# The sign of float64 weight words: from VectorE's integer operations to a parametric ReLU of ScalarE

## Chip, cores and metric

One core of one Trainium2 chip runs the kernel. The metric is the device time of one execution in microseconds (us), the median of 3 runs for the kernel before. A profile of one execution shows the five engines: PE (TensorE, its matmuls), PEld (its weight loads), DVE (VectorE), ACT (ScalarE), POOL (GpSimd) and SP (SyncE, which here only issues DMAs).

## What is computed

An attention layer and two feed-forward layers, one after the other, on 2 x 576 = 1152 tokens of width 512:

```
q_pool = q.reshape(B, H, S // 2, 2, D).mean(axis=3)          # B=2, H=8, S=1152, D=64
attn = softmax(q_pool @ k.T / sqrt(D)) ; x = attn @ v        # x: 1152 x 512
xn = x / sqrt(mean(x*x) + 1e-6) * rms_g                      # first layer, d_ff = 1536
x = (silu(xn @ w_gate) * (xn @ w_val)) @ w_out
h = x @ w_in                                                 # second layer, d_ff = 2048
out = (h * tanh(softplus(h))) @ w_out2                       # h*tanh(softplus(h)) is Mish
```

The five weight matrices (`w_gate`, `w_val`, `w_out`, `w_in`, `w_out2`) arrive as float64, everything else as float32. TensorE is given float16 pairs: each operand is split into a high and a low part, and each product is three matmuls (high x high, high x low, low x high).

## The kernel before

**Weights.** A float64 is two 32-bit words. A job (there are 68) loads a tile `raw` of 128 x 512 pairs of words, 512 KB, and turns it into the float16 pair, in four steps that lie on three engines:

- `w_a` on ACT: the high word, read as a float32 with every second word of `raw` skipped, times 2^-111, into `gx`. That leaves the sign in bit 31 and brings the exponent to where a shift by 3 puts it in float32's place.
- `w_b` on DVE, three integer operations on 128 x 512 words: L408 shifts `gx` left by 3 and masks off bit 31, L411 takes the sign bit from `gx` and ors it in, L414 shifts the low word right by 29 and ors it in. The result `c` holds the bits of the float32.
- `w_c`: ACT (L421) rounds `c` to float16 (the high part), POOL (L134) subtracts it from `c` for the low part.

The tiles `raw` have 4 buffers, `gx` and `c` 2 each. An engine works through its instructions in the order of the program. `job_step` issues `w_c` of one job, `w_b` of the next and `w_a` of the one after that, so a job crosses three steps.

**Stages.** The 72 attention steps (`attn_step`) come first: scores on PE (L249), row maximum on DVE (`m`, L267), exponential on ACT (`e`, L274), high part on ACT (L287) and low part on POOL, a DMA transpose, and five steps later the product with v on PE. From step 54 on, the first four jobs are spread over the steps by `job_piece`, one piece a step, four steps a job: `w_a` (with `w_c` of the job before), L408, L411, L414.

Then come the first layer's units (`unit1`): 24 matmuls of 288 columns for one block of 128 features and 288 tokens, ACT's Silu (L572), DVE's product `fo` (L574), ACT's high part (L581) and POOL's low part `h`. After each unit stands one `job_step`; PE can be three units ahead, since the units take two of six PSUM banks each. The jobs run out before the units do. The output matmuls of the first layer (`unit1o`, 36 matmuls each, DVE's `y` at L136 frees the bank) again have one or two job steps behind each; `w_out`'s blocks (`woh`) have two buffers, so a job for a third block waits until PE is done with the first, and what stands behind it on ACT, POOL and DVE waits too.

In the second layer's loop one step is 12 matmuls into `z`, Mish on ACT (`mo`, L648), the high part of `g` on ACT, the low part on DVE (L136), one job step while there are jobs (the 16 of `w_out2`, `w2o_job`), and from the seventh step on the output matmuls `po`. `z` has five PSUM banks.

Of the kernel before, what the change touches and what calls it, by code (L numbers as in the profile page):

```python
# [9 lines left out]
F32 = mybir.dt.float32  # L10
F16 = mybir.dt.float16
I32 = mybir.dt.int32
ACTF = mybir.ActivationFunctionType
ALU = mybir.AluOpType
# [26 lines left out]
def kernel(  # L41
# [13 lines left out]
    nc = tc.nc  # L55
# [48 lines left out]
    w2o = stretch.rearrange("p (k w d) -> p k w d", k=F2, w=2)  # L104
# [280 lines left out]
    def words(w):  # L385
        return w.bitcast(I32)
# [3 lines left out]
    def w_load(src, n):  # L390
        t = raw_p.tile([128, n, 128 * KD // n, 2], I32, tag="raw", name="raw", bufs=4)
        weng[0].dma_start(out=t, in_=src)
        return t

    def w_a(job):
        t = job["raw"]
        gx = raw_p.tile([128, t.shape[1], t.shape[2]], F32, tag="gx", name="gx")
        nc.scalar.activation(out=gx, in_=t[:, :, :, 1].bitcast(F32), func=ACTF.Copy, scale=2.0 ** -111)
        job["g"] = gx

    def w_b(job, part=None):

        t, g = job["raw"], job["g"].bitcast(I32)
        if part in (None, 0):
            job["c"] = raw_p.tile([128, t.shape[1], t.shape[2]], I32, tag="c", name="c")
        c = job["c"]
        if part in (None, 0):
            nc.vector.tensor_scalar(out=c, in0=g, scalar1=3, scalar2=0x7FFFFFFF,  # L408
                                    op0=ALU.logical_shift_left, op1=ALU.bitwise_and)
        if part in (None, 1):  # L410
            nc.vector.scalar_tensor_tensor(out=c, in0=g, scalar=-0x80000000, in1=c,  # L411
                                           op0=ALU.bitwise_and, op1=ALU.bitwise_or)
        if part in (None, 2):
            nc.vector.scalar_tensor_tensor(out=c, in0=t[:, :, :, 0], scalar=29, in1=c,  # L414
                                           op0=ALU.logical_shift_right, op1=ALU.bitwise_or)
            del job["raw"], job["g"]

    def w_c(job):
        hi, lo = job["to"]()
        cf = job.pop("c").bitcast(F32)  # L420
        nc.scalar.activation(out=hi, in_=cf, func=ACTF.Copy)  # L421
        lo_op(job.get("eng", nc.gpsimd), lo, cf, 1.0, hi)

    jobs = []
    jn = [0, 0, 0, 0]

    def job_load(upto):
        while jn[0] < min(upto, len(jobs)):
            jobs[jn[0]]["raw"] = jobs[jn[0]]["load"]()
            jn[0] += 1  # L430
# [3 lines left out]
    def job_step(k=1):  # L434

        for _ in range(k):
            if jn[3] < jn[2]:
                w_c(jobs[jn[3]])
                jn[3] += 1
            if jn[2] < jn[1]:  # L440
                w_b(jobs[jn[2]])
                jn[2] += 1
            if jn[1] < len(jobs):
                job_load(jn[1] + 1)
                w_a(jobs[jn[1]])
                jn[1] += 1
            job_load(jn[1] + AHEAD)

    def job_piece(k):

        i, p = divmod(k, 4)
        if p == 0 and i:
            w_c(jobs[i - 1])
            jn[3] += 1
        if i == NE:
            return
        if p == 0:
            w_a(jobs[i])
            jn[1] += 1
            job_load(jn[1] + AHEAD)  # L460
        elif p == 1:
            w_b(jobs[i], 0)
        else:
            w_b(jobs[i], p - 1)
            jn[2] += p == 3


    ss_t, rw = {}, {}
# [158 lines left out]
    def w2o_job(z):  # L627
        return {"load": lambda: w_load(words(w_out2)[z * 128:(z + 1) * 128, :].rearrange(
            "(k p) (f t) -> p k f t", p=128, t=2), 1),
            "to": lambda: (w2o[:, z:z + 1, 0, :], w2o[:, z:z + 1, 1, :])}  # L630

    gt, zt = {}, {}

# [123 lines left out]
    with tc.manual_schedule():  # L757
# [25 lines left out]
        for n in range(NIT):  # L783
            attn_step(n)
            if rs:
                rs.pop(0)()
            if n == RMS0:
                rs = rms_steps(0, 0, NI + 1, 2)
            if n == JOBL:
                job_load(AHEAD)  # L790
            if 0 <= n - JOB0 <= 4 * NE:
                job_piece(n - JOB0)
# [84 lines left out]
        for i, (d, c) in enumerate(outs):  # L877
# [4 lines left out]
            if i:  # L882
                unit1o_end(*outs[i - 1])
        unit1o_end(*outs[-1])
        jobs += [w2o_job(z) for z in range(F2)]
        for p in (ps_f, ps_t, ps_av, wo_p, h1_p, h0_p, ftm):
            p.release()
# [60 lines left out]
```

## Time and profile before

| | |
|---|---|
| median of 3 runs | 677.12 us (676.36 to 677.2) |
| span of the profiled execution | 674.8 us |
| what lies around the span, median less span | 2.3 us |
| PE busy | 605.0 us (90%) |
| DVE busy | 449.9 us (67%) |
| ACT busy | 392.4 us (58%) |
| POOL busy | 328.3 us (49%) |

The times are those of the page of the profile. Matmuls overlap in it (their ends are modelled), so PE's share says where it works, not whether it works at its full rate; the count of matmuls in a stretch says that. The share of DVE is an average over stages: it is near full in some stretches and near nothing in others. An engine's time includes time in which an instruction has started and waits for a port.

### The profile page before, as it was taken

Reading aid. Unit: us, or ns where it says so; the run is one execution under the profiler, and the core shown is the slowest. Engines: PE = TensorE matmul, PEld = TensorE weight load, DVE = VectorE, ACT = ScalarE, POOL = GpSimd, SP = SyncE. Lnnn points to the kernel's source line nnn. Section 1 sums busy time; section 2 is a strip of 40 time slices with the busy share of each in tenths; the row PEclk is TensorE's granted clock in tenths of the full one; section 3 lists DMA queues with packets and bytes.
Section 4 is the critical chain, followed back from the end, with each engine's and each line's share of the span. In section 5 each row is a group of like instructions: output and inputs, shape, how many; then the busy total and the mean of one; then the engine's idle time right before and its main releaser. Section 6 shows DMA issues by size and latency. Waiting matters only on the chain.

```text
span 674.8 us, 14672 instructions
## 1 busy us (share of the span) xinstructions
PE 605.0 (90%) x5880; PEld 421.6 (62%) x5880; DVE 449.9 (67%) x740; ACT 392.4 (58%) x659; POOL 328.3 (49%) x260
## 2 busy tenths in 40 slices
PE   3688888888867788899999999999999999999997
PEld 2466566666645567677777677777755555555553
DVE  3889998989969996769999922488299911111110
ACT  4888898998968887655555541344356623223221
POOL 0778878688889752467878741344133300000000
PEclk9899999999988899999999999999999999999999
DMA  6799999999998997625555512156055101001001
GB/s 190 123 211 189 186 183 185 197 182 186 204 203 163 174 161 147 132 94 157 159 157 169 158 47 63 39 182 187 17 169 159 64 0 48 1 1 32 16 1 47
DMA packets 161908, 84.05 MB, mean 125 GB/s; under 512 B 124720, under 2 KB 152368, under 8 KB 161840
## 3 DMA queue, kind: packets, MB, share of 16 engines
q1 hardware_dynamic: 151184, 67.71, 47.0%
q10 hardware_dynamic: 10656, 15.40, 8.4%
q8 instruction: 46, 0.75, 0.5%
q14 instruction: 22, 0.18, 0.1%
HBM read 50.07 MB, written 2.36 MB: 78 GB/s over the span
## 4 chain that ended last, share of the span: by engine, by line
PE 49%; DVE 28%; ACT 8%; issue 8%; DMA 4%; POOL 2%; ACTq 1%; SPq 0%; DVEq 0%; POOLq 0%
DVE m L267 8%; DVE c L411 6%; PE z L544 5%; PE z L546 5%; PE z L545 5%; PE po L681 4%; PE po L680 4%; PE po L679 4%; ACT e L274 3%; PE py L544 3%; PE py L546 3%; PE py L545 3%; DVE c L408 3%; DMA et<-hl 3%; DVE et L134 2%
## 5 line engine op out<-in xcount | busy, mean ns | idle before, releaser
L134 POOL TENSOR_TENSOR hl<-e,hl 128x768 f16<-128x768 f32 x71 | 117.5, 1655 | 60.5 <-ACT hl L287 37.0
L267 DVE TENSOR_REDUCE m<-s 128x1 f32<-128x1152 f32 x72 | 97.3, 1351 | 8.9 <-PE s L249 7.6
L274 ACT ACTIVATE e<-s,m 128x1152 f32<-128x1152 f32 x72 | 87.7, 1218 | 18.8 <-DVE m L268 17.6
L249 PE MATMUL s<-kqT 128*128 128x384 f16 (+1 forms) x480 | 87.9, 336 | 9.6 <-DVE kqT L203 7.5
L136 DVE SCALAR_TENSOR_TENSOR g<-mo,g 128x384 f16<-128x384 f32 x48 | 26.9, 562 | 100.5 <-ACT g L654 100.5
L411 DVE SCALAR_TENSOR_TENSOR c<-gx,c 128x512 int32<-128x512 int32 x68 | 75.7, 1114 | 2.2
L338 PE MATMUL av<-vv,et 128*128 128x65 f16 (+1 forms) x720 | 75.4, 195 | 1.8 <-DMA et<-hl 1.0
L134 POOL TENSOR_TENSOR stretch<-c,stretch 128x512 f16<-128x512 f32 x40 | 51.3, 1283 | 52.0 <-ACT stretch L421 51.8
L414 DVE SCALAR_TENSOR_TENSOR c<-raw,c 128x512 int32<-128x512 int32 x68 | 75.0, 1103 | 2.2
L340 PE MATMUL av<-vv,et 128*128 128x64 f16 (+1 forms) x720 | 75.3, 194 | 0.0
L341 PE MATMUL av<-vv,et 128*128 128x65 f16 (+1 forms) x720 | 75.1, 196 | 0.0
L338 PEld LDWEIGHTS <-et 128*128 128x128 f16 (+1 forms) x720 | 68.0, 102 | 3.6 <-issue 2.3
L340 PEld LDWEIGHTS <-et 128*128 128x128 f16 (+1 forms) x720 | 67.8, 101 | 0.8
L341 PEld LDWEIGHTS <-et 128*128 128x128 f16 (+1 forms) x720 | 67.8, 101 | 0.0
L134 POOL TENSOR_TENSOR h<-fo,h 128x288 f16<-128x288 f32 x48 | 48.8, 1016 | 36.3 <-ACT h L581 36.3
L648 ACT ACTIVATE mo<-z 128x384 f32<-128x384 f32 x48 | 23.3, 484 | 71.3 <-PE z L546 71.3
L287 ACT ACTIVATE hl<-e 128x768 f16<-128x768 f32 x72 | 60.7, 843 | 3.5 <-DMA et<-hl 1.4
L544 PE MATMUL z<-y,w2i 128*128 128x384 f16 x192 | 62.6, 326 | 0.0
L545 PE MATMUL z<-y,w2i 128*128 128x384 f16 x192 | 62.6, 326 | 0.0
L546 PE MATMUL z<-y,w2i 128*128 128x384 f16 x192 | 62.6, 326 | 0.0
L309 PE MATMUL ep<-idf,e 128*128 128x128 f32 x216 | 39.0, 291 | 24.7 <-ACT e L274 23.5
L249 PEld LDWEIGHTS <-kqT 128*128 128x128 f16 (+1 forms) x480 | 40.2, 102 | 33.1 <-issue 15.6
(106 smaller groups left out, 1570.0 us busy)
## 6 DMA issues: line engine op xcount, KB each, us to landing
raw<-in_moe_w_out_dram SPq DMA_DIRECT2D x28, 512.0 KB, 3.4
raw<-in_moe_w_in_dram SPq DMA_DIRECT2D x16, 512.0 KB, 3.7
raw<-in_moe_w_gate_dram SPq DMA_DIRECT2D x8, 512.0 KB, 3.6
raw<-in_moe_w_val_dram SPq DMA_DIRECT2D x8, 512.0 KB, 3.5
vn<-in_v_dram ACTq DMA_DIRECT2D x14, 288.0 KB, 2.9
kn<-in_k_dram ACTq DMA_DIRECT2D x12, 288.0 KB, 4.5
qn<-in_q_dram ACTq DMA_DIRECT2D x12, 256.0 KB, 3.4
raw<-in_moe_w_gate_dram ACTq DMA_DIRECT2D x4, 512.0 KB, 5.0
```

The source lines that it names most:

```text
L134: eng.tensor_tensor(out=out_, in0=in_, in1=hi, op=ALU.subtract)
L249: mm = nc.tensor.matmul(out=ps[p0:p0 + m, c, 0:SN], lhsT=qt[:, w * NTI + slot, p0:p0 + m], rhs=kt[:, e * NJ + c * per:e * NJ + (c + 1) * p ...
L267: nc.vector.tensor_reduce(out=m[:, 0:1], in_=ps[:, :, 0:SN], op=ALU.max, axis=AXL.XY, negate=True)
L274: nc.scalar.activation(out=e.rearrange("p (c s) -> p c s", c=SC), in_=ps[:, :, 0:SN], func=ACTF.Exp, bias=m[:, 1:2], scale=s_scale)
L338: nc.tensor.matmul(out=av[0:m, o0:o0 + D + 1], lhsT=hi, rhs=vr[:, D:2 * D + 1], start=(jj == 0), stop=False)
L340: nc.tensor.matmul(out=av[0:m, o0:o0 + D], lhsT=hi, rhs=vr[:, 0:D], start=False, stop=False)
L341: nc.tensor.matmul(out=av[0:m, o0:o0 + D + 1], lhsT=et[:, z + (NB if jj < NB else PB), p0:p0 + m], rhs=vr[:, D:2 * D + 1], start=False, st ...
L411: nc.vector.scalar_tensor_tensor(out=c, in0=g, scalar=-0x80000000, in1=c, op0=ALU.bitwise_and, op1=ALU.bitwise_or)
L414: nc.vector.scalar_tensor_tensor(out=c, in0=t[:, :, :, 0], scalar=29, in1=c, op0=ALU.logical_shift_right, op1=ALU.bitwise_or)
L544: nc.tensor.matmul(out=ps, lhsT=w0, rhs=x0, start=(i == 0), stop=False)
L545: nc.tensor.matmul(out=ps, lhsT=w0, rhs=x1, start=False, stop=False)
L546: nc.tensor.matmul(out=ps, lhsT=w1, rhs=x0, start=False, stop=(i == n - 1))
```

## The change

The 52 jobs of the first four weight matrices lose one of their three DVE operations. ACT's pass over the high word becomes a parametric ReLU: positive words are multiplied by 2^-111 as before, negative ones by 2^-111 and by -2^32, so that they come out positive with 32 added to the exponent, which is bit 28. The shift by 3 puts this bit where the sign belongs, and what was masked off and ored in needs no operation of its own. DVE's first operation now reads `raw` (the low word, shifted right by 29), its second shifts `gx` left by 3 and ors `c` in. In the attention's `job_piece` the fourth step of a job has no DVE operation any more.

The 16 jobs of `w_out2`, which run beside Mish, are marked `"mish"`: they keep ACT's plain scaled copy and get four DVE operations (low word shifted; sign masked and ored in; `gx` shifted and masked in place; the two ored).

```diff
     def w_a(job):
...
-        nc.scalar.activation(out=gx, in_=t[:, :, :, 1].bitcast(F32), func=ACTF.Copy, scale=2.0 ** -111)
+        hw = t[:, :, :, 1].bitcast(F32)
+        if job.get("mish"):
+            nc.scalar.activation(out=gx, in_=hw, func=ACTF.Copy, scale=2.0 ** -111)
+        else:
+            nc.scalar.activation(out=gx, in_=hw, func=ACTF.Prelu, scale=2.0 ** -111, alpha=-(2.0 ** 32))
     def w_b(job, part=None):
...
         if part in (None, 0):
-            nc.vector.tensor_scalar(out=c, in0=g, scalar1=3, scalar2=0x7FFFFFFF,
-                                    op0=ALU.logical_shift_left, op1=ALU.bitwise_and)
+            nc.vector.tensor_scalar(out=c, in0=t[:, :, :, 0], scalar1=29, scalar2=None,
+                                    op0=ALU.logical_shift_right)
         if part in (None, 1):
-            nc.vector.scalar_tensor_tensor(out=c, in0=g, scalar=-0x80000000, in1=c,
-                                           op0=ALU.bitwise_and, op1=ALU.bitwise_or)
-        if part in (None, 2):
-            nc.vector.scalar_tensor_tensor(out=c, in0=t[:, :, :, 0], scalar=29, in1=c,
-                                           op0=ALU.logical_shift_right, op1=ALU.bitwise_or)
+            if job.get("mish"):
+                nc.vector.scalar_tensor_tensor(out=c, in0=g, scalar=-0x80000000, in1=c,
+                                               op0=ALU.bitwise_and, op1=ALU.bitwise_or)
+                nc.vector.tensor_scalar(out=g, in0=g, scalar1=3, scalar2=0x7FFFFFFF,
+                                        op0=ALU.logical_shift_left, op1=ALU.bitwise_and)
+                nc.vector.tensor_tensor(out=c, in0=g, in1=c, op=ALU.bitwise_or)
+            else:
+                nc.vector.scalar_tensor_tensor(out=c, in0=g, scalar=3, in1=c,
+                                               op0=ALU.logical_shift_left, op1=ALU.bitwise_or)
...
     def job_piece(k):
...
-        elif p == 1:
-            w_b(jobs[i], 0)
-        else:
+        elif p < 3:
             w_b(jobs[i], p - 1)
-            jn[2] += p == 3
+            jn[2] += p == 2
...
-            "to": lambda: (w2o[:, z:z + 1, 0, :], w2o[:, z:z + 1, 1, :])}
+            "to": lambda: (w2o[:, z:z + 1, 0, :], w2o[:, z:z + 1, 1, :]), "mish": True}
```

Lines move by some places: in the changed kernel L414 is the first operation (`c<-raw`), L424 the second; L418, L420 and L422 are the other three of the marked jobs. PE, POOL, SP and the order on ACT are as before, and ACT has the same five table loads at the same places.

On DVE, the second half of the first job in the attention, before (m is the row maximum, et, r and x belong to the attention's product, kqT to the next heads' transposes):

```order
L411 SCALAR_TENSOR_TENSOR c<-gx,c 128x512
L267 TENSOR_REDUCE m<-s 128x1
L268 TENSOR_SCALAR m<-m 128x1
L134 TENSOR_TENSOR et<-ep,et 128x384
L361 TENSOR_SCALAR r<-av 128x2
L373 RECIPROCAL r<-r 128x2
L375 TENSOR_TENSOR x<-av,r 128x128
L414 SCALAR_TENSOR_TENSOR c<-raw,c 128x512
L267 TENSOR_REDUCE m<-s 128x1
L268 TENSOR_SCALAR m<-m 128x1
L203 COPY kqT<-s 128x1024
```

The same place in the changed kernel:

```order
L424 SCALAR_TENSOR_TENSOR c<-gx,c 128x512
L267 TENSOR_REDUCE m<-s 128x1
L268 TENSOR_SCALAR m<-m 128x1
L134 TENSOR_TENSOR et<-ep,et 128x384
L361 TENSOR_SCALAR r<-av 128x2
L373 RECIPROCAL r<-r 128x2
L375 TENSOR_TENSOR x<-av,r 128x128
L267 TENSOR_REDUCE m<-s 128x1
L268 TENSOR_SCALAR m<-m 128x1
L203 COPY kqT<-s 128x1024
```

The job's last operation is gone ahead of a row maximum; this happens in four of the steps.

On DVE in the first layer's units, before, two units with a job each between their products fo:

```order
L574 SCALAR_TENSOR_TENSOR fo<-ft,pv 128x288
L408 TENSOR_SCALAR c<-gx 128x512
L411 SCALAR_TENSOR_TENSOR c<-gx,c 128x512
L414 SCALAR_TENSOR_TENSOR c<-raw,c 128x512
L574 SCALAR_TENSOR_TENSOR fo<-ft,pv 128x288
```

And in the changed kernel:

```order
L582 SCALAR_TENSOR_TENSOR fo<-ft,pv 128x288
L414 TENSOR_SCALAR c<-raw 128x512
L424 SCALAR_TENSOR_TENSOR c<-gx,c 128x512
L582 SCALAR_TENSOR_TENSOR fo<-ft,pv 128x288
L414 TENSOR_SCALAR c<-raw 128x512
```

Two operations stand between two products instead of three, and the first of them reads raw and no longer ACT's gx.

On DVE in the second layer's loop, before, the last of `w_out2`'s jobs between two low parts of g:

```order
L414 SCALAR_TENSOR_TENSOR c<-raw,c 128x512
L136 SCALAR_TENSOR_TENSOR g<-mo,g 128x384
L408 TENSOR_SCALAR c<-gx 128x512
L411 SCALAR_TENSOR_TENSOR c<-gx,c 128x512
L414 SCALAR_TENSOR_TENSOR c<-raw,c 128x512
L136 SCALAR_TENSOR_TENSOR g<-mo,g 128x384 x33
```

And in the changed kernel:

```order
L422 TENSOR_TENSOR c<-gx,c 128x512
L136 SCALAR_TENSOR_TENSOR g<-mo,g 128x384
L414 TENSOR_SCALAR c<-raw 128x512
L418 SCALAR_TENSOR_TENSOR c<-gx,c 128x512
L420 TENSOR_SCALAR gx<-gx 128x512
L422 TENSOR_TENSOR c<-gx,c 128x512
L136 SCALAR_TENSOR_TENSOR g<-mo,g 128x384 x33
```

Here one operation has come in, L420, ahead of the last one of each job.

## Rows read from the trace of the kernel before

**Rows 1.** Windows: stretch, length, busy of PE, PEld, DVE, ACT, POOL; clock, DMA:

```profile
300.00:350.00 50.00, 50.00 (x410) 39.94 (x409) 48.94 (x63) 28.15 (x62) 38.71 (x31) 1.00 0.51 159
350.00:390.00 40.00, 37.61 (x296) 28.66 (x295) 38.32 (x47) 21.76 (x49) 31.00 (x25) 1.00 0.51 159
...
488.00:538.00 50.00, 50.00 (x281) 27.23 (x279) 48.90 (x63) 30.58 (x62) 18.66 (x16) 1.00 0.43 137
```

**Rows 2.** Waits of PE in 280:300, 345:390, 440:470: total, times, longest:

```profile
PE pv L546 <- POOL stretch L134: 1.2, 1, 1.2
...
PE pv L544 <- DVE fo L574: 2.3, 5, 0.5
...
PE py L544 <- DVE y L136: 1.9, 2, 1.0
```

**Rows 3.** Timeline of DVE in the first layer's units: start, us, instruction:

```profile
375.44 0.44 DVE L574 SCALAR_TENSOR_TENSOR fo<-ft,pv 128x288 f32<-128x288 f32 x1
...
379.45 0.41 DVE L408 TENSOR_SCALAR c<-gx 128x512 int32<-128x512 int32 x1
379.90 0.69 DVE L411 SCALAR_TENSOR_TENSOR c<-gx,c 128x512 int32<-128x512 int32 x1
...
382.07 0.44 DVE L574 SCALAR_TENSOR_TENSOR fo<-ft,pv 128x288 f32<-128x288 f32 x1
```

**Rows 4.** Timeline of POOL, a low part of h and one of a weight:

```profile
286.89 0.73 POOL L134 TENSOR_TENSOR h<-fo,h 128x288 f16<-128x288 f32 x1 [0.33 <-ACT h L581]
...
491.33 1.16 POOL L134 TENSOR_TENSOR stretch<-c,stretch 128x512 f16<-128x512 f32 x1 [2.02 <-ACT stretch L421]
```

**Rows 5.** Chain that ended last, DVE's third operation of the attention's jobs, first and last:

```profile
207.93 0.73 DVE c L414
...
250.54 0.87 DVE c L414
```

**Rows 6.** Timeline of ACT, the exponentials behind these operations, with their idle time before:

```profile
211.50 1.21 ACT L274 ACTIVATE e<-s,m 128x1152 f32<-128x1152 f32 x1
...
227.73 1.22 ACT L274 ACTIVATE e<-s,m 128x1152 f32<-128x1152 f32 x1 [0.20 <-DVE m L268]
...
240.35 1.22 ACT L274 ACTIVATE e<-s,m 128x1152 f32<-128x1152 f32 x1 [0.37 <-DVE m L268]
...
252.96 1.22 ACT L274 ACTIVATE e<-s,m 128x1152 f32<-128x1152 f32 x1 [0.34 <-DVE m L268]
```

**Rows 7.** Timeline of DVE in the attention, the first operation of the second job:

```profile
215.41 3.07 DVE L408 TENSOR_SCALAR c<-gx 128x512 int32<-128x512 int32 x1
```

**Rows 8.** Timeline of DVE in the first layer's output stage:

```profile
448.63 1.37 DVE L408 TENSOR_SCALAR c<-gx 128x512 int32<-128x512 int32 x1 [1.47 <-POOL woh L134]
...
451.37 0.45 DVE L136 SCALAR_TENSOR_TENSOR y<-py,y 128x288 f16<-128x288 f32 x1
```

**Rows 9.** Timelines of DVE, ACT and PE in the second layer's loop:

```profile
491.43 1.61 DVE L411 SCALAR_TENSOR_TENSOR c<-gx,c 128x512 int32<-128x512 int32 x1
...
494.61 1.61 DVE L411 SCALAR_TENSOR_TENSOR c<-gx,c 128x512 int32<-128x512 int32 x1
...
491.74 0.47 ACT L648 ACTIVATE mo<-z 128x384 f32<-128x384 f32 x1
...
497.59 0.33 PE L544 MATMUL z<-y,w2i 128*128 128x384 f16 x1
...
536.51 0.33 PE L544 MATMUL z<-y,w2i 128*128 128x384 f16 x1
```

**Rows 10.** Groups by line: instruction, count, busy us, mean ns, idle before:

```profile
L398 ACT ACTIVATE gx<-raw 128x512 f32<-128x512 f32 x68 | 45.1, 666 | 0.0
...
L141 DVE TENSOR_SCALAR vn<-vn 128x1152 f32<-128x1152 f32 x7 | 5.3, 753 | 0.0
L481 ACT ACTIVATE sq<-x 128x512 f32<-128x512 f32 x8 | 5.0, 626 | 4.5 <-DVE x L375 4.5
...
L572 ACT ACT_TABLE_LOAD x2 | 2.6, 1283 | 0.0
```

## The prediction

> **What bounds the kernel now.** The page's slices come first: from the middle of the span on PE is full nearly everywhere, ahead of that DVE, ACT and POOL are. Only PE's idle time can be won back in the later part, so the windows are read for counts, not for busy time. In 300:350 PE starts 410 matmuls in 50 us, 8.2 a us, which is its rate at 288 columns (0.122 us each, 24 x 0.122 = 2.93 us a unit). In 350:390 it starts 296 where that rate gives 328: 32 x 0.122 = 3.9 us are lost [rows 1]. DVE is busy nearly all the time in both [rows 1]. The waits then name what PE lost time to after the attention: once a weight's low part from POOL (1.2 us), five times DVE's product fo (2.3 us by that view, the larger part of the 3.9), twice DVE's y (1.9 us) [rows 2]. So about 7 us are lost behind the attention, all in stages with weight jobs, and PE is the bound elsewhere there.
>
> The timeline shows why DVE is late in the units. Two products fo with two jobs between them are 6.63 us apart, 3.31 us a unit against PE's 2.93 [rows 3]. DVE and POOL take turns: in the second layer an L411 that starts at 491.43 while POOL works from 491.33 to 492.49 takes 1.61 us, and ends 0.55 us after POOL, where the same operation takes 0.69 us alone [rows 3, 4, 9]. The Trainium skill says so in "SBUF — State Buffer", section "Who interferes with whom": a VectorE operation with two SBUF inputs, or one in a two-port mode, excludes a GpSimd operation that reads SBUF, and the later one blocks fully. The trace agrees on the exclusion; by the rule alone the hold times would add, and below the sum is made both ways.
>
> In the attention the chain of waits puts DVE's third operation on the path in all four jobs, 0.73 to 0.87 us each [rows 5]. ACT's own timeline says less, and is used here: the exponential behind these operations has waited for the row maximum 0 (no idle time shown at 211.50), 0.20, 0.37 and 0.34 us [rows 6]. That is all by which an earlier row maximum can move it; then ACT's queue is the bound.
>
> **The change, part by part.** *Attention.* Four of DVE's third operations go. By ACT's idle time that is 0 + 0.20 + 0.37 + 0.34 = 0.9 us. Bounds: 3.3 us if the chain is right (four of 0.73 to 0.87). On the other side stands a turn lost to POOL: DVE's first operation of the second job took 3.07 us instead of 0.41 [rows 3, 7], because POOL got its next operation in first. Which way such a turn falls after the change can't be read from the trace; one more of half that size costs 1.3 us, so the low end is -0.4. I take 0.9.
>
> *The parametric ReLU.* No row has one. Nearest are ACT's squares of 512 contiguous elements at 626 ns (with a sum), beside 666 ns for the scaled copy out of every second word [rows 10]: another function costs no more per element. I take 0; the upper bound is some 0.1 us for each of the four passes in the attention, where ACT is the bound, and nothing in the units, where ACT is busy 28 of 50 us [rows 1].
>
> *DVE's first operation reads every second word of raw.* The nearest row is the scaling of v, which works on every second float32: 1152 elements in 753 ns, 0.65 ns each [rows 10]. L408 takes 0.41 us for 512 [rows 3], about the same rate beside a fixed part. So I take 0.41 us; the bound above is the 0.69 us of an operation at L411's rate. It no longer waits for ACT's gx, the second operation does.
>
> *The late weight ahead of the units.* POOL's low part, for which PE waits 1.2 us, stands behind an L414 that costs 0.69 us or more. Without it the chain is shorter by that, and by a turn at POOL's port where it waited; 1.2 us, bounds 0.7 and 1.2.
>
> *Units.* Per unit the port is held by L408 (0.41), L411 (0.69), L414 (taken as 0.69, L411's time), h (0.73) and a weight's low part (1.16): 3.68 us by adding, 3.31 measured [rows 3, 4]. Without L414 the sum is 2.99 by adding, which is an upper bound; scaled by 3.31/3.68 it is 2.69. What PE needs is less than 2.93 only if it has no lead. It has one: about 28 units have a job, DVE fell behind by 0.38 in each, 10.6 us in all, and PE lost 3.9 of these; the rest, 6.7 us, its banks absorbed. So PE loses nothing as long as a unit takes DVE and POOL less than 2.93 + 6.7/28 = 3.17 us. Both sums are below. All 3.9 us come back; the lower bound is 2, where one gap in two stays.
>
> *Output stage of the first layer.* DVE stands at 448.63 behind POOL's `woh` and then has three operations ahead of y, which ends at 451.82 [rows 8]. That wait comes from PE's use of the block's buffer and stays. One operation less (0.69 us) brings the first of the two waits down by that, and the next y has two jobs and so two operations less, 1.4 us, which covers the rest. Of 1.9 us I take 1.5, since the first wait is not covered whole; bounds 0.7 and 1.9.
>
> *Second layer.* Here one operation comes in per job: L420, like L408 0.41 us, 0.45 from start to start [rows 3]. DVE's period is 494.61 - 491.43 = 3.18 us a job, so 3.63 after; with the low words at the slow rate 3.9. PE's own step is (536.51 - 497.59)/10 = 3.89 us, and its eighth `z` starts at 497.59, 5.4 us after the Mish that has to free its bank, the third (492.21) [rows 9]. Over 14 more steps PE therefore waits only if a job takes over 3.89 + 5.4/14 = 4.27 us. What hides the 16 operations is this lead and PE's output matmuls; a job that takes more costs 14 us for each us over 4.27. I take 0.
>
> **Sum.** 0.9 + 1.2 + 3.9 + 1.5 = 7.5 us off the profiled execution, whose span of 674.8 and 2.3 around it are the median of 677.1: **669.6 us**. The bounds give -0.4 + 0.7 + 2.0 + 0.7 = 3.0 and 3.3 + 1.2 + 3.9 + 1.9 = 10.3, that is 674.1 and 666.8.
>
> **The rivals.** *The chain of waits is right in the attention:* each removed operation shortens the path by its whole length, 3.3 us instead of 0.9: 667.2. For it: DVE is on that chain throughout. Against: ACT's queue [rows 6].
>
> *The port stays the bound:* POOL's turns come out badly and a unit stays at 3.25 us, so that 28 x 0.08 = 2.2 us of the 3.9 remain, and in the attention a turn is lost (1.3 us instead of a gain of 0.9, 2.2 in all): 674.0. Against it stands that even the plain sum of hold times is 2.99.
>
> *The four operations of the second layer:* slower than before, if a job of `w_out2` takes more than 4.27 + 7.5/14 = 4.81 us; at 5.0 us PE loses 10.2, and the time is 679.8. That needs 1.8 us for one operation more, as if two of DVE's operations lost a turn to POOL in each job. POOL has one operation per job there (16 in 488:538, [rows 1]) of 1.16 us, so one turn is all that can be lost; even with both single-input operations at the slow rate a job takes 4.2.
>
> *The change does not do what it says, the new function being in none of the table sets loaded.* A table load takes 1.28 us [rows 10]; two a unit on ACT (28.15 us of busy time in 17 units, 1.66 each) would make 4.2 us a unit, so that PE loses 28 x (4.2 - 3.17) = 29 us in place of 3.9: 677.1 - 3.6 + 25 = 698.6. The Trainium skill, "ScalarE activation tables: per-element evaluation and per-set limits", section "What a function is on this engine", gives the same 1283 ns and says that two functions in one set need no switch. Against the rival: the changed order on ACT has the same five loads.
>
> *Nothing to measure:* PE's regained lead is lost at the next wait for `woh`. Behind 470 no wait of PE is left that could take it, so 677 has little for it.
>
> **How the numbers follow.** Chances: forecast 0.66 (its own range 667.5 to 672), chain right 0.14, port still the bound 0.10, nothing 0.04, second layer 0.05, table loads 0.01. The range that holds the time 8 times in 10 takes in the forecast, the chain's case and most of the port's: 666.3 to 673.5. Less than 0.2% (1.35 us) is what a measurement of this kernel can't tell from no change. Faster by more: 0.66 + 0.14 + 0.10 = 0.90; same 0.04; slower 0.06.
>
> **What would show it.** In the profile after: 24 matmuls each 2.93 us without gaps from the first unit with jobs to the output stage, DVE with idle time ahead of fo; no wait of PE for fo; at most 0.7 us for y; the first operation on `raw` at 0.4 us when alone; ACT's pass over the high words at 0.67 us; in the second layer 3.6 us a job and no wait of PE for `mo` or `z`. The attention should end about 1 us earlier. The forecast is wrong if the last step of the attention moves by more than 2 us either way, if a unit still takes DVE over 3.17 us, or if the time between the first `z` and the end grows.

## The result and the profile after

The changed kernel takes 668.22 us (median of 4 runs, 666.69 to 669.41) against 677.16 for the kernel before in the same session: a ratio of 0.986, with a 95% interval of 0.9835 to 0.9884. The forecast was 669.6, in a range of 666.3 to 673.5. The profiled execution spans 666.1 us, 8.7 less than before.

The windows of the changed kernel, over stretches that answer to those of before (length, busy of PE, PEld, DVE, ACT, POOL; clock, DMA):

```profile
300.00:350.00 50.00, 50.00 (x410) 39.94 (x409) 43.15 (x53) 33.07 (x69) 36.64 (x34) 1.00 0.56 179
350.00:390.00 40.00, 40.00 (x329) 31.94 (x328) 23.69 (x31) 20.31 (x43) 23.76 (x24) 1.00 0.38 121
480.00:530.00 50.00, 50.00 (x280) 27.18 (x279) 48.59 (x70) 26.93 (x55) 15.51 (x14) 1.00 0.40 127
```

In 350:390 PE starts 329 matmuls in place of 296 [rows 1], which is its full rate: 33 x 0.122 = 4.0 us. DVE is busy for 23.7 us of this stretch in place of 38.3, in part because its last job beside the units now ends at 374.4 and no longer at 388.7. In the second layer PE starts as many matmuls in 50 us as before (280 and 281).

All that PE waited for after the attention, from 270 to 470 (total, times, longest):

```profile
PE pg L552 <- DMA stretch<-xh: 1.6, 1, 1.6
PE pg L552 <- ACT ft L580: 0.5, 1, 0.5
PE py L552 <- DVE y L136: 0.2, 1, 0.2
```

The first two stand ahead of the units and are in the trace of before too, 0.5 and 1.6 us. Of the waits in [rows 2], that for the weight's low part and the five for `fo` are gone, and of 1.9 us for `y` 0.2 are left.

The timeline of DVE in the changed kernel (start, us, instruction, idle time before it): the attention's second job, two units, the second layer.

```profile
214.87 3.07 DVE L414 TENSOR_SCALAR c<-raw 128x512 int32<-128x512 int32 x1
...
330.88 0.46 DVE L582 SCALAR_TENSOR_TENSOR fo<-ft,pv 128x288 f32<-128x288 f32 x1
331.25 0.42 DVE L414 TENSOR_SCALAR c<-raw 128x512 int32<-128x512 int32 x1
331.71 1.53 DVE L424 SCALAR_TENSOR_TENSOR c<-gx,c 128x512 int32<-128x512 int32 x1
333.82 0.45 DVE L582 SCALAR_TENSOR_TENSOR fo<-ft,pv 128x288 f32<-128x288 f32 x1 [0.58 <-PE pv L554]
334.19 1.23 DVE L414 TENSOR_SCALAR c<-raw 128x512 int32<-128x512 int32 x1
335.46 1.10 DVE L424 SCALAR_TENSOR_TENSOR c<-gx,c 128x512 int32<-128x512 int32 x1
336.76 0.46 DVE L582 SCALAR_TENSOR_TENSOR fo<-ft,pv 128x288 f32<-128x288 f32 x1 [0.20 <-PE pv L554]
...
483.04 1.61 DVE L418 SCALAR_TENSOR_TENSOR c<-gx,c 128x512 int32<-128x512 int32 x1
...
486.68 1.61 DVE L418 SCALAR_TENSOR_TENSOR c<-gx,c 128x512 int32<-128x512 int32 x1
```

Two units take (336.76 - 330.88)/2 = 2.94 us each, PE's own pace, and DVE waits for PE ahead of `fo` (0.58 and 0.20 us) instead of PE for DVE [rows 3]. Without these waits two units take DVE 5.88 - 0.78 = 5.10 us, 2.55 each, its waits for POOL included. The operation on every second word of `raw` takes 0.42 us where nothing is in its way. A job of the second layer takes 486.68 - 483.04 = 3.64 us.

The timeline of ACT in the attention, exponentials from step 55 on, the first behind ACT's pass of the first job, to the last (and one `et`, the operation ahead of an exponential):

```profile
196.63 1.21 ACT L274 ACTIVATE e<-s,m 128x1152 f32<-128x1152 f32 x1
...
226.88 1.21 ACT L274 ACTIVATE e<-s,m 128x1152 f32<-128x1152 f32 x1
...
238.65 0.47 ACT L314 ACTIVATE et<-ep 128x384 f16<-128x384 f32 x1
239.02 1.21 ACT L274 ACTIVATE e<-s,m 128x1152 f32<-128x1152 f32 x1
...
251.20 1.22 ACT L274 ACTIVATE e<-s,m 128x1152 f32<-128x1152 f32 x1
...
254.54 1.23 ACT L274 ACTIVATE e<-s,m 128x1152 f32<-128x1152 f32 x1
```

The three that answer to 227.73, 240.35 and 252.96 in [rows 6] no longer wait for the row maximum. The same places in the kernel before:

```profile
197.17 1.21 ACT L274 ACTIVATE e<-s,m 128x1152 f32<-128x1152 f32 x1
...
239.51 0.47 ACT L314 ACTIVATE et<-ep 128x384 f16<-128x384 f32 x1
...
256.32 1.22 ACT L274 ACTIVATE e<-s,m 128x1152 f32<-128x1152 f32 x1
```

From the first exponential to the last are 57.91 us, before 59.15. So 1.24 of the 8.7 us come from here, and 0.54 from ahead of the first of these exponentials. Up to there the two kernels differ only in the function of one ACT pass (0.66 us before, 0.67 after), and that start lies between 195.91 and 199.71 us over the runs of this study: the 0.54 is scatter. The remaining 6.9 us come from behind the attention: from the start of the last exponential to the end of the span are 666.1 - 254.54 = 411.56 us, before 418.48.

### The profile page after: what moved, and what is told of

It reads as the page before. It is cut to its first block, busy times and chain, and to the rows that moved or that the text cites. A ratio compares the mean times of both kernels' runs of the same rounds, so it can differ in the third digit from the quotient of the medians.

```text
span 666.1 us, 14636 instructions
## 1 busy us (share of the span) xinstructions
PE 604.1 (91%) x5880; PEld 422.3 (63%) x5880; DVE 418.2 (63%) x704; ACT 395.4 (59%) x659; POOL 315.2 (47%) x260
## 4 chain that ended last, share of the span: by engine, by line
PE 64%; DVE 17%; ACT 11%; issue 3%; POOL 2%; DMA 2%; ACTq 1%; SPq 0%; DVEq 0%; POOLq 0%
DVE m L267 7%; PE z L552 5%; PE z L553 5%; PE z L554 5%; PE po L689 5%; PE po L688 5%; PE po L687 5%; ACT e L274 4%; PE pg L552 3%; PE pg L554 3%; PE pv L554 3%; PE pv L553 3%; PE pv L552 3%; PE pg L553 3%; PE py L552 3%
## 5 line engine op out<-in xcount | busy, mean ns | idle before, releaser
L134 POOL TENSOR_TENSOR stretch<-c,stretch 128x512 f16<-128x512 f32 x40 | 47.2, 1179 | 56.2 <-ACT stretch L431 55.9
L414 DVE TENSOR_SCALAR c<-raw 128x512 int32<-128x512 int32 x68 | 52.2, 767 | 26.6 <-POOL woh L134 24.4
L134 POOL TENSOR_TENSOR h<-fo,h 128x288 f16<-128x288 f32 x48 | 45.4, 946 | 43.7 <-ACT h L589 43.7
L424 DVE SCALAR_TENSOR_TENSOR c<-gx,c 128x512 int32<-128x512 int32 x52 | 56.6, 1088 | 3.0 <-ACT gx L404 1.1
```

What stands on the lines that cost most here:

```text
L134: eng.tensor_tensor(out=out_, in0=in_, in1=hi, op=ALU.subtract)
L424: nc.vector.scalar_tensor_tensor(out=c, in0=g, scalar=3, in1=c, op0=ALU.logical_shift_left, op1=ALU.bitwise_or)
```

## The experiments

Two lengths scatter far less than the medians and are given below beside them, each from the one profiled execution of a kernel. From the exponential at 211.50 in [rows 6] (210.96 in the changed kernel) to the last are 44.82 us before and 43.58 changed; in all nine kernels that have the changed order in the attention, 43.55 to 43.62. The "rest" is the length from the last exponential to the end: 418.48 us before, 411.56 changed.

Diffs are against the changed kernel, cut to the lines that matter. Each time is a median of 6 runs, of 12 in `one_input` and `two_inputs`; the kernel before had medians of 676.38, 676.82 and 676.47 us in the three sessions.

**The changed kernel again.**

> The changed kernel once more, as the measure for the other runs of this call. Both theories expect 668.2 us within 1.3.

668.13 us, ratio 0.9876 (0.9853 to 0.99). Its exponentials lie 253.78 - 195.91 = 57.87 us apart, and its rest is 411.52.

**Attention: the old three operations for its four jobs.**

```diff
-        if job.get("mish"):
+        if job.get("mish") or job.get("three"):
...
+            if part in (None, 2):
+                nc.vector.scalar_tensor_tensor(out=c, in0=t[:, :, :, 0], scalar=29, in1=c,
+                                               op0=ALU.logical_shift_right, op1=ALU.bitwise_or)
...
+        for job in jobs[:NE]:
+            job["three"] = True
```

> The four jobs of the attention get the three old operations back, all other jobs stay changed. ACT-queue theory: what the third operation costs there is only ACT's idle time behind it, so the time is 0.9 to 1.3 us over the changed kernel, and the exponential behind the third operation shows 0 to 0.4 us of idle time in each job. Chain theory: the whole operation counts, 3.3 us over the changed kernel. If the gain of the change lies mainly in the attention and not with PE's waits, it is over 5 us.

669.96 us, ratio 0.9902 (0.9876 to 0.9928): 1.8 more than the changed kernel beside it. ACT's exponentials in this kernel:

```profile
198.15 1.21 ACT L274 ACTIVATE e<-s,m 128x1152 f32<-128x1152 f32 x1
...
228.70 1.22 ACT L274 ACTIVATE e<-s,m 128x1152 f32<-128x1152 f32 x1 [0.21 <-DVE m L268]
...
241.31 1.22 ACT L274 ACTIVATE e<-s,m 128x1152 f32<-128x1152 f32 x1 [0.36 <-DVE m L268]
...
253.93 1.22 ACT L274 ACTIVATE e<-s,m 128x1152 f32<-128x1152 f32 x1 [0.34 <-DVE m L268]
...
257.28 1.22 ACT L274 ACTIVATE e<-s,m 128x1152 f32<-128x1152 f32 x1
```

The waits of [rows 6] are back, and the stretch is 59.13 us again. The four operations cost 59.13 - 57.87 = 1.26 us. From step 55 this stretch has some scatter of its own (58.28 us in `second_three`, which has the changed attention); the shorter one is 44.81 us here, 1.2 to 1.3 over the nine. The rest is 411.52. The chain of waits, by which the operations are worth 3.3, is refuted; the sum of ACT's idle times (0.9) was 0.3 short.

**Second layer: the old three operations for `w_out2`.**

```diff
+        if job.get("mish"):
...
+                nc.vector.tensor_scalar(out=c, in0=g, scalar1=3, scalar2=0x7FFFFFFF,
+                                        op0=ALU.logical_shift_left, op1=ALU.bitwise_and)
...
+            return
```

> The 16 jobs of the second layer get the three old operations back. Theory of the hidden fourth operation: the period of a job falls from 3.64 to 3.18 us and the time does not move (0 within 0.7 us of the changed kernel), since PE waits for neither z nor g in either. Rival, that the added operation costs its own time: 16 x 0.45 = 7 us less than the changed kernel.

668.5 us, ratio 0.9874 (0.9849 to 0.99). The jobs are 3.18 us apart again instead of 3.64, PE waits for nothing in either kernel from 470 to the end, and the time stays (the rest is 411.53 us): the added operation is hidden.

**ACT's parametric ReLU or a copy.**

```diff
-            nc.scalar.activation(out=gx, in_=hw, func=ACTF.Prelu, scale=2.0 ** -111, alpha=-(2.0 ** 32))
+            nc.scalar.activation(out=gx, in_=hw, func=ACTF.Copy, scale=2.0 ** -111)
```

> The parametric ReLU of the 52 jobs becomes the scaled copy again, with nothing else changed, so the weights of these jobs lose their sign. Theory that the function costs nothing: 666 to 670 ns for one such pass in both, time equal to the changed kernel within 0.7 us. Rival, that it is slower than a copy: each pass 0.09 us shorter or more than in the changed kernel, and 0.4 us or more off the time through the attention.

This kernel leaves out the sign of these weights. 668.7 us, ratio 0.9886 (0.986 to 0.9912), and a rest of 411.51. Its group of the pass over the high words (count, busy us, mean ns, idle before):

```profile
L404 ACT ACTIVATE gx<-raw 128x512 f32<-128x512 f32 x52 | 34.4, 666 | 0.0
```

The same line of the changed kernel has a mean of 665 ns. The function costs nothing over a copy.

**One operation more per job behind the attention, with two SBUF inputs.** If the gain there comes from one operation less, this gives it back.

```diff
+                if not job.get("attn"):
+                    nc.vector.tensor_tensor(out=c, in0=c, in1=c, op=ALU.bitwise_or)
...
+        for job in jobs[:NE]:
+            job["attn"] = True
```

> The same place, the same length, but an operation with both inputs in SBUF (c or c, which changes nothing): the old third operation's cost put back behind the attention and nothing else. Port theory and busy-time theory both expect the old losses: about 3.9 us in the units, 1.2 at the late weight, 1.5 at y, so 674 to 676 us. If it stays at 668 the gain lay elsewhere (the attention, or the release of the weights' buffers).

675.92 us, ratio 0.999 (0.9975 to 1.0005). Its waits of PE from 270 to 470:

```profile
PE pv L554 <- DVE fo L584: 2.3, 5, 0.5
PE py L554 <- DVE y L136: 2.0, 2, 1.1
...
PE pv L556 <- POOL stretch L134: 1.2, 1, 1.2
```

Those are the three waits of [rows 2], with their counts, and the rest is 418.60 us, as before the change. The whole gain behind the attention is this one operation per job; that DVE's first operation now reads `raw` and does not wait for ACT's `gx` brings nothing there by itself.

**The same with one SBUF input.** A reduction over `c` takes DVE as long, but reads one tile. By the prediction's reason, the port's time that adds up, it should cost nothing in the units.

```diff
+                if not job.get("attn"):
+                    u = raw_p.tile([128, 1], F32, tag="u", name="u")
+                    nc.vector.tensor_reduce(out=u, in_=c.bitcast(F32), op=ALU.max, axis=AXL.XY)
```

> After the two operations of each of the 48 jobs behind the attention DVE makes one more pass over the same 512 words, a maximum with one input in SBUF, whose result nobody reads. Port theory (DVE and POOL take turns for operations that hold the shared port, and this one does not): a unit stays at 2.94 us or near it, PE loses under 1 us in the units, the time is the changed kernel's 668.2 within 1.5 us. Rival, that DVE's busy time as such was the bound: three operations again make 3.2 to 3.3 us a unit, PE loses 2 to 4 us, the time is 671 to 674.

674.85 us, ratio 0.9974 (0.9958 to 0.9989). It costs nearly as much as the other (a rest of 418.11 us), more than either theory expected of the time, and the prediction's reason falls. One unit on DVE in this kernel:

```profile
319.72 0.44 DVE L585 SCALAR_TENSOR_TENSOR fo<-ft,pv 128x288 f32<-128x288 f32 x1
320.08 1.24 DVE L414 TENSOR_SCALAR c<-raw 128x512 int32<-128x512 int32 x1
321.35 1.10 DVE L424 SCALAR_TENSOR_TENSOR c<-gx,c 128x512 int32<-128x512 int32 x1
322.49 0.69 DVE L428 TENSOR_REDUCE u<-c 128x1 f32<-128x512 f32 x1
323.09 0.45 DVE L585 SCALAR_TENSOR_TENSOR fo<-ft,pv 128x288 f32<-128x288 f32 x1
```

And POOL beside it:

```profile
319.88 1.16 POOL L134 TENSOR_TENSOR stretch<-c,stretch 128x512 f16<-128x512 f32 x1 [1.35 <-ACT stretch L434]
321.00 0.91 POOL L134 TENSOR_TENSOR h<-fo,h 128x288 f16<-128x288 f32 x1
323.20 1.16 POOL L134 TENSOR_TENSOR woh<-c,woh 128x512 f16<-128x512 f32 x1 [1.29 <-ACT woh L434]
```

A unit takes 3.37 us here, and PE waits for `fo` twelve times, 3.0 us in all. Yet POOL, the other user of the port, is idle for 1.3 us of every unit, and the operations that wait for each other (L414, L424 and POOL's two) add up to 0.42 + 0.69 + 0.73 + 1.16 = 3.0 us, not 3.37. What happens instead: L424's end releases ACT's high part, and that POOL's low part of the same weight; when DVE is through with the reduction and `fo` and comes to L414, POOL is in the middle of it (L414 1.24 us instead of 0.42). `fo` releases `h` in the same way, and L424 meets that one (1.10 instead of 0.69). In this kernel DVE meets both operations of POOL in every unit. A unit takes DVE its own work plus these two waits, 0.8 + 0.4 = 1.2 us: 3.37 = 2.15 + 1.22. Without the reduction (0.60 from start to start) that is 2.77, under PE's 2.93. How the waits fall differs between kernels. Before the change units of two kinds take turns (3.64 and 2.99 us from 375.44 on), and in two units DVE waits 0.2, 0.9, 0.4 and 0.8 us, 1.2 a unit again. In the changed kernel, where DVE has idle time, L424 waits alone in one unit (1.53 us) and both operations in the next (1.23 and 1.10).

The Trainium skill, "SBUF — State Buffer", section "Who interferes with whom", says that a reduction never contends with GpSimd. The trace agrees for the operation itself: three of the 47 recorded overlap an operation of POOL, by up to 0.56 us, and take 0.69 us like all others. In most units it runs while POOL is idle; the unit grew by its length all the same, since the waits around it stayed.

**Two theories for that.** New theory: each POOL operation that needs the port costs DVE one wait. Rival: a unit's time goes with the number of DVE's operations. The kernel of `two_inputs`, with one of POOL's two operations moved to ACT (a copy, so the low part of h is not computed):

```diff
-        lo_op(nc.gpsimd, h[:, f, 1, cs], o, 1.0, h[:, f, 0, cs])
+        nc.scalar.activation(out=h[:, f, 1, cs], in_=o, func=ACTF.Copy)
```

> As the run with the extra operation of two inputs, but the low part of h comes from ScalarE as a second copy and no longer from POOL (it is then not the low part: what is left out is the subtraction). POOL has one operation per unit left, that of the weight. Theory of the turns (a unit takes DVE its own 2.26 us of work plus the time for which DVE's operations wait until POOL's are done, 1.05 us): the waits fall to the weight's 0.84 or less, a unit takes 3.0 to 3.1 us, which PE's lead covers, and PE loses under 1 us in the units instead of 3.9; time 671 to 673. Rival, that DVE's count of operations sets the unit: 3.3 us a unit, 3.9 us lost, 675 to 676.

672.73 us, ratio 0.994 (0.9919 to 0.9962). One unit on DVE:

```profile
320.22 0.44 DVE L584 SCALAR_TENSOR_TENSOR fo<-ft,pv 128x288 f32<-128x288 f32 x1
320.58 0.41 DVE L414 TENSOR_SCALAR c<-raw 128x512 int32<-128x512 int32 x1
321.03 0.69 DVE L424 SCALAR_TENSOR_TENSOR c<-gx,c 128x512 int32<-128x512 int32 x1
321.75 1.53 DVE L427 TENSOR_TENSOR c<-c 128x512 int32<-128x512 int32 x1
323.21 0.44 DVE L584 SCALAR_TENSOR_TENSOR fo<-ft,pv 128x288 f32<-128x288 f32 x1
```

One operation per unit waits now (1.53 us instead of 0.69), a unit takes 2.99 with all four DVE operations, and PE starts 329 matmuls in 350:390, as many as without the added one. So the count of DVE's operations does not set it. The new theory fits, but this run alone does not single it out: the plain sum of hold times, 0.41 + 0.69 + 0.69 + 1.16 = 2.95 us, fits as well, and it is `one_input` that rules that sum out. The run also bears out the prediction's reading of PE's lead: 2.99 us a unit is over PE's 2.93 and under 3.17, and PE loses nothing in the units. The waits for `y` stay (2.0 us), as the output stage still has the operation, and 0.7 us of the one for the late weight.

**Second layer, two operations more per job, to find where it would turn.**

```diff
+                for _ in range(2):
+                    nc.vector.tensor_tensor(out=c, in0=c, in1=c, op=ALU.bitwise_or)
```

> Two more operations with both inputs in SBUF in each of the second layer's 16 jobs. The period of a job should go from 3.64 to 5.1 us. Theory of the lead (nothing lost up to 4.27 us a job, 14 us for each us above): PE waits 11.6 us, time 678 to 681. Rival, that the operations are hidden as before: 668. Rival, that each counts in full: 16 x 1.46 = 23 us, 691.

684.74 us, ratio 1.0118 (1.0096 to 1.014). DVE's jobs are as far apart as worked out, 5.09 us:

```profile
500.02 0.42 DVE L414 TENSOR_SCALAR c<-raw 128x512 int32<-128x512 int32 x1
...
505.11 0.42 DVE L414 TENSOR_SCALAR c<-raw 128x512 int32<-128x512 int32 x1
```

But PE's waits from 470 on are others than the prediction named:

```profile
PE po L690 <- POOL stretch L134: 5.2, 7, 0.9
PE po L689 <- ACT stretch L433: 3.9, 4, 1.2
```

PE waits for the weights' own parts ahead of `po`, not for Mish and a bank of `z`. From the first matmul of this loop to the last are 678.40 - 475.93 = 202.47 us, in the changed kernel 661.82 - 475.19 = 186.63: 15.8 us are lost, where 14 x (5.09 - 4.27) = 11.5 would have been by the prediction's threshold. Spread over 14 steps that puts the threshold near 5.09 - 15.8/14 = 4.0 us, little over PE's own step. This is an estimate, and it has a second cause in it. The waits shown are 9.1 us; in three stretches behind a wait PE also worked at a lower granted clock, which this window has at 0.91 on the mean:

```profile
500.00:520.00 20.00, 16.84 (x80) 8.25 (x79) 19.31 (x29) 7.62 (x16) 4.63 (x4) 0.91 0.33 106
```

In 513:514 it is 0.50, the level of 1.2 GHz, after PE had waited 1.21 and 0.86 us from 508.94 on, and matmuls into `z` start 0.32 us apart instead of 0.16. The windows 520:540 and 540:560 have 0.91 too, so some 3 x 20 x 0.09 = 5.4 us of work at full speed are missing. PE still keeps step with the jobs (four steps from 512.19 to 532.52, 5.08 us each), so these losses may stand where there would have been waits otherwise; no run tells which.

**Two attempts at more.** `y_first` issues the previous block's `y` ahead of the job steps, for the last 0.2 us and DVE's queue before it:

```diff
+            if i:
+                unit1o_end(*outs[i - 1])
...
-            if i:
-                unit1o_end(*outs[i - 1])
```

> In the first layer's output stage DVE's and ACT's y of the unit before is issued ahead of the job steps and not behind them. Theory: the 0.2 to 0.6 us that PE still waits for y there go, the time is 0.5 us under the changed kernel, no wait of PE for y is left. Rival, that the weights of the jobs behind it come later and PE waits for those: equal or some tenths slower.

669.16 us, ratio 0.9887 (0.9863 to 0.991). PE no longer waits for `y`, but the median is not below the changed kernel's. The rest shows the gain: 410.96 us here and 410.99 in `early_y` below, against 411.51 to 411.56 in six kernels with the old order (the changed one, `after_again`, `attn_three`, `second_three`, `all_copy`, `early_first`). The 0.55 us are what was expected, and less than the scatter of the attention.

`early_first` issues the strided operation, which needs no result of ACT, one step earlier in the attention:

```diff
-        elif p < 3:
-            w_b(jobs[i], p - 1)
-            jn[2] += p == 2
+            w_b(jobs[i], 0)
+        elif p == 2:
+            w_b(jobs[i], 1)
+            jn[2] += 1
```

> In the attention the first operation of a job (it no longer needs ACT's gx) is issued one step earlier, in the step in which ACT has the two passes of the jobs and is the bound. Theory of ACT's queue: DVE's operation is then hidden there; of the idle time of ACT that stood behind it (0.93, 1.58, 0.86 and 0.86 us before four exponentials in the changed kernel) most goes, 1.5 to 3 us off the attention, 665 to 667 us. Rival, that DVE meets POOL's queue there just as well and delays the row maximum behind it: the same time as the changed kernel or slower.

670.33 us, ratio 0.9911 (0.9893 to 0.9929): slower than the changed kernel by 2. Its exponentials from step 55 to the last are 256.76 - 196.90 = 59.86 us apart, 1.95 more, and its rest is 411.54, so all of it comes from the attention. DVE's second operation of the second job in this kernel:

```profile
219.14 4.48 DVE L424 SCALAR_TENSOR_TENSOR c<-gx,c 128x512 int32<-128x512 int32 x1
```

POOL's operations around it:

```profile
218.56 1.67 POOL L134 TENSOR_TENSOR xh<-xn,xh 64x512 f16<-64x512 f32 x1
220.20 1.63 POOL L134 TENSOR_TENSOR hl<-e,hl 128x768 f16<-128x768 f32 x1
221.77 0.17 POOL L149 MEMSET vv<- 128x18 f16 x1
221.84 1.23 POOL L134 TENSOR_TENSOR vv<-vn,vv 128x576 f16<-128x576 f32 x1
```

ACT's exponential behind it:

```profile
225.17 1.22 ACT L274 ACTIVATE e<-s,m 128x1152 f32<-128x1152 f32 x1 [4.74 <-DVE m L268]
```

The first operations of the last three jobs now cost 0.53 to 0.61 us, as meant (the first job's 1.17), but the second job's second one arrived while POOL had several in a row, waited for all of them, and the exponential stood still for 4.74 us.

> The first operation one step earlier, as in the run beside it, and y ahead of the job steps in the output stage. Theory: both add, 0.6 us under the run with the first alone, no wait of PE for y. Rival: they do not.

Both attempts together: 670.16 us, ratio 0.9912 (0.9891 to 0.9933), with the same 4.48 us operation. By the median no version beat the changed kernel.

## Why the prediction was right, and where its reason was not

*What bounds the kernel:* held. PE, waiting only in the stages with jobs, and by the amounts read from the windows and waits.

*Attention, 0.9 us:* the mechanism held, the size was 1.24 (1.26 in `attn_three`). The sum of idle times is 0.1 us short at each of three exponentials. With no wait the exponential starts 239.02 - 238.65 = 0.37 us after `et` does, though `et` is shown with 0.47; with the wait it starts 240.35 - 239.51 = 0.84 after it, of which 0.37 are shown as idle. So 0.47 came back there and not 0.37. The lost turn of 3.07 us stayed where it was [rows 7].

*Parametric ReLU, 0, and strided operation, 0.41 us:* held (665 against 666 ns; 0.42).

*Late weight, 1.2 us:* held, the wait is gone. The 6.9 us behind the attention less 4.0 in the units and 1.7 at `y` leave 1.2 for it.

*Units, 3.9 us:* the amount held, the reason failed. The step "Per unit the port is held by L408, L411, L414, h and a weight's low part" took the hold times as what adds up. `one_input` added an operation that holds no port and got 3.37 us a unit. In its place: DVE's own work plus one wait for each POOL operation that it meets. Without L414 the prediction's way gives 2.69 or 2.99 us, the waits give at most 2.77 and 2.55 was measured; all are under 3.17, so the forecast came out the same, and that the reason did no harm here was luck: the operation taken out both held the port and took DVE's time. For an operation with one input they differ, and there the prediction's step would have been wrong by what PE loses in the units of `one_input`, 4.9 us (40 matmuls fewer in 350:390).

*PE's lead, 3.17 us a unit:* not contradicted: 2.99 goes without a loss, 3.31 and 3.37 with one. No run lies between, so the 3.17 itself isn't shown.

*Output stage, 1.5 of 1.9 us:* 1.7.

*Second layer, 3.63 us a job and hidden:* held, 3.64. The threshold of 4.27 us had the wrong wait in it: it was taken from Mish and the banks of `z`, but the weights' parts come late first (`second_six`), by the estimate above near 4.0. At 3.64 that did not matter.

*The sum, 7.5 against 8.7 us:* 0.54 of the difference is scatter ahead of the first job, 0.3 the attention, the rest the stages behind it.

## What to carry to other kernels

When VectorE and GpSimd release each other's work, count the GpSimd operations that each pass of VectorE meets, and charge a wait for each; do not add up the port's hold times. In three kernels here (before, `one_input`, `low_on_scalar`) this gives the measured unit, with waits read from their own rows. As long as VectorE sets the pace, an operation removed from such a chain returns its length even if it never held the port, and one moved to another place can meet a longer GpSimd queue. Where ACT's queue sets the pace, its idle times price a VectorE operation better than the chain of waits does (0.9 and 3.3 for 1.24 here).

## What the runs showed that was not expected

An operation of VectorE that is ready can stand behind several of GpSimd's in a row, not one: 4.48 us for an operation of 0.69, behind three with the port and a memset that followed without a gap.

The attention's scatter is larger than its effects here: the exponential of step 55 starts anywhere from 195.91 to 199.71 us in kernels whose instructions up to there are the same, while what lies behind the attention repeats within 0.1 us (411.51 to 411.56 in six kernels).

Behind waits PE also worked at a lower clock: in `second_six` the granted clock stood at 0.50 after two waits of 1.21 and 0.86 us, and matmuls started twice as far apart until it rose again. The waits alone don't show that loss.
